# Moving one product and three preparation steps at the hand-over from the written order to the visits

## The chip, the cores and the metric

The kernel runs on one core of one Trainium2 chip. The metric is the device time of one execution in microseconds (us); lower is better. Several runs of the same kernel are taken, and their median is compared. A profile of one further execution shows what each engine did and when.

## The reference

The program chains a recurrent attention block (RetNet) and a feed-forward block with SiLU. All tensors are float32, apart from the weights, which the host hands over as 64-bit floats and the kernel reads as pairs of 32-bit words.

```python
# q, k, v: (B, H, S, D) = (4, 8, 768, 64); w_in: (512, 2048); w_out: (2048, 512)
gamma = 1.0 - 2.0 ** (-5.0 - np.arange(H))
for t in range(S):
    state = gamma[None, :, None, None] * state + einsum('bhd,bhe->bhde', k[:, :, t], v[:, :, t])
    y[:, :, t] = einsum('bhd,bhde->bhe', q[:, :, t], state) / sqrt(D)
x = y.transpose(0, 2, 1, 3).reshape(B * S, H * D)     # 3072 tokens x 512
h = x @ w_in
out = (h * sigmoid(h)) @ w_out
```

## The kernel before

**Tiling.** The sequence is cut into 6 chunks of 128 positions. A *unit* is one chunk of one of the 4 batches: units 0 to 3 are chunk 0, units 4 to 7 are chunk 1, and so on to unit 23. The four units of a chunk make a *group* of 512 tokens, whose x is one tile `xt[c]`. w_in is cut into 16 *slices* of 128 columns. A *product* (c, f) multiplies group c's x by slice f; (1, 0) is group 1 and slice 0.

**Precision.** Each float32 operand is split into three parts, so a product is three groups of four matmuls of 128x512: four for the high part, four for the low part (both add up in the bank `ha`), four for the third part (bank `hb`), all at L645. The x of a unit is split by `split_x`: high part on ScalarE (ACT, L552), low part on VectorE (DVE, L555), third part on DVE (L558). A slice of w_in is first turned from 64-bit to 32-bit floats (`convert_steps`: L196 on ACT, then L199 to L217 on DVE) and then split (`split_steps`: L120 on ACT, L123 on DVE, L126 on ACT, L128 on DVE).

**What a unit goes through.** Its k and q are turned on TensorE (PE) by `stage_t`, called T (L436: `kp` and `qp`), and copied out by ACT (L438). SC makes the scores and the sums (L462, L452), A masks them (L470), adds the state (L478, L482), and Q scales q (L403). `stage_y`, called YA and YB, makes the output y (L501) in two halves. X takes y out (L539, tile `ys`) and splits it into x. K (L398 on DVE) or KA (eight small multiplications on ACT) scales k. A *visit* m in `halves(m)` does T of unit m and the first half of y of unit m-2; after a `yield` it does SC and A of unit m-1, the second half of y and X of unit m-2, issues loads, and handles slices of w_in.

**A product's close.** `close_steps` takes `ha` out on ACT (L655), subtracts `hb` on DVE (L660) and applies SiLU on ACT (L665). The result is a tile `g`; `put_g` writes it to DRAM (L671), from where a second phase reads it back for the multiplication by w_out.

**Shared buffers.** Three PSUM banks, taken in turn by `turn`, hold every `kp`, `ha` and `hb`, so each tile waits until the one three places before it has been read. `qp` has one bank of its own. Three SBUF buffers (`hpool`) hold every `g` and every `ys` in turn, so each waits for the store, or the reader, of the one three places before it. Two landing buffers hold raw slices of w_in; the conversion works in one buffer of each kind.

**What sets the order.** PE runs in the order in which the source calls it. For the other engines the order is the source's as well up to `early_order.close()`; after that a scheduler at build time orders them, with `queue(...)` as hints. The written part ends with T(9), KA(9), the steps of unit 8, X(7), and `begin_w()` for slice 3. From there the list `pairs` names six products with a half visit behind each: `next(half_visits)` runs the first half of visit 10 ahead of the list, and then each product of `pairs` is followed by the next half; the last is followed by the whole of visit 13. The list `three` goes on from there.

**Slices 3 to 6.** `begin_w()` issues a slice's load ahead (two slices on) and its conversion; `end_w()`, called in the next visit, issues its split. Slice 3 is begun in the written part.

```python
        if EARLY + 2 <= m < 3 * B + 2:      # visits 10 to 13
            with queue(masked[0]):
                end_w()
                if EARLY + 2 < m:           # from visit 11
                    begin_w()
```

So visit 10 ends slice 3; visits 11, 12 and 13 begin slices 4, 5 and 6, and visit 12 ends slice 4, visit 13 slice 5. The product (0, 4) stands behind visit 12.

Of the kernel before, what the change touches and what calls it, by code (L numbers as in the profile page):

```python
# [33 lines left out]
def kernel(  # L34
# [29 lines left out]
    B, H, S, D = q.shape  # L64
# [5 lines left out]
    NF = DF // 128  # L70
# [60 lines left out]
    def split_w(*of):  # L131
        steps = split_steps(*of)
        next(steps)
        yield
        list(steps)
# [4 lines left out]
    EARLY = 2 * B  # L140
# [4 lines left out]
    def load(name, n):  # L145
        if n >= len(units):
            return
        c, b = units[n]
        src = {"k": k, "q": q, "v": v}[name]
        if n < EARLY:  # L150

            if n not in early:
                early[n] = wpool.tile([128, 3, H, D], FP32, tag=f"w{4 + n}", name=f"kqv_{n}")
            t = early[n][:, "kqv".index(name)]
        else:
            t = ld.tile([128, H, D], FP32, tag=f"{name}f", name=f"{name}f_{n}",
                        bufs=2 if name == "q" else 3)
        nc.sync.dma_start(out=t, in_=src[b, :, ds(c * C, C)].rearrange("h t d -> t h d"))
        kqv[name][n] = t
# [60 lines left out]
    def convert_w(i):  # L220

        if i + W_AHEAD not in staged:
            load_w(i + W_AHEAD)
        out = []
        steps = convert_steps(i, out)
        for _ in range(6):
            next(steps, None)

        def rounded():
            list(steps)  # L230
            return out[0]

        return rounded
# [53 lines left out]
    def begin_w():  # L287

        i = taken[0]
        taken[0] += 1  # L290
        split = split_w(i, convert_w(i)(), "wi", scale, w_sb, True)
        next(split)
        half_split.append(split)
# [135 lines left out]
    def stage_t(n):  # L429

        for name, to, bufs, src, tp in (
                ("kt", kt, 2, kqv["k"][n], turn(f"kp_{n}")),
                ("qt", qt, 3, kqv["q"].pop(n), banks("q", f"qp_{n}", 1)[:, 0])):
            tp = tp.rearrange("p (a t) -> p a t", a=HP)
            for a in range(HP):
                nc.tensor.transpose(tp[:, a, :], src[:, 2 * a : 2 * a + 2, :], ident)  # L436
            to[n] = one.tile([128, HP, C], FP32, tag=name, name=f"{name}_{n}", bufs=bufs)
            evac[:] = [nc.scalar.copy(out=to[n], in_=tp).ins]  # L438

    def score_tile(n):  # L440
        u = banks("s", f"sc_{n}")
        sc, sums = (u[:, :, ts(i, 4 * D)].rearrange("p o (a t) -> p o a t", a=HP)
                    for i in range(2))
        return sc, sums

    def stage_s(n, sums):

        kf, vs = kqv["k"].pop(n), kqv["v"][n]
        for a in range(HP):
            for o in range(2 if units[n][0] < NC - 1 else 1):  # L450
                for j in range(2):
                    nc.tensor.matmul(sums[ts(j, D), o, a, :], lhsT=kf[ts(o, D), 2 * a + j, :],  # L452
                                     rhs=vs[ts(o, D), 2 * a + j, :], start=True, stop=True,
                                     skip_group_check=True)
# [36 lines left out]
    def stage_y(n):  # L491

        vs, amn, qtn = kqv["v"].pop(n), am.pop(n), qt.pop(n)
        states = steps_of.pop(n)
        yp = banks("y", f"y_{n}")[:, :, : 4 * D].rearrange("p o (a t) -> p o a t", a=HP)

        started, done, new = set(), [], []

        def product(a, o, j, lhsT, rhs):
            e = j ^ (a % 2)  # L500
            i = nc.tensor.matmul(yp[ts(e, D), o, a, :], lhsT=lhsT, rhs=rhs,  # L501
                                 start=(e, o) not in started, stop=True,
                                 skip_group_check=True).ins
            started.add((e, o))
            if new:
                fence(done[-1], i)
                new.clear()
            done.append(i)

        def scores():  # L510
            for a in range(HP):
                for o in range(2):
                    for j in range(2):
                        product(a, o, j, vs[ts(o, D), 2 * a + j, :], amn[ts(o, D), j, a, :])

        def states_with(part):

            new.extend([part] * part)
            for a in range(HP):
                for o in range(2):  # L520
                    j = o ^ part
                    if states[o] is not None:
                        product(a, o, j, states[o][ts(j, D), a, :], qtn[ts(j, D), a, ts(o, D)])

        return scores, states_with, yp
# [67 lines left out]
    def halves(m):  # L593

        first, mid, last = (0 <= m - i < len(units) for i in range(3))
        if first and m < FAR:
            stage_t(m)
        if last:
            scores, states_with, yp = stage_y(m - 2)
            scores()  # L600
            states_with(0)
        yield
        if mid:
            sc, sums = score_tile(m - 1)
            stage_s(m - 1, sums)
            stage_a(m - 1, sc)
            if 1 < m <= 3 * B + 1 and units[m - 1][1] == 0:
                next_chunk()

            with queue(taken_out[0]) if m > 3 * B + 1 else ExitStack():  # L610
                finish_a(m - 1, sc, sums)
            scale_q(m - 1)
            if m > 3 * B + 1 and units[m - 1][1] == B - 1:

                behind_copy.append(next_chunk)
        if first and m < FAR:
            scale_k(m)
        if last:
            states_with(1)
            finish_y(m - 2, yp)  # L620

        if FAR <= m < len(units):
            with queue(fenced[0]):
                part_t(m)
        for name in "kqv":
            for n in (m + 1, m + 2):
                if n >= EARLY and n == (m + 1 if name == "v" or n > FAR else m + 2):
                    load(name, n)
        if EARLY + 2 <= m < 3 * B + 2:
            with queue(masked[0]):  # L630
                end_w()
                if EARLY + 2 < m:
                    begin_w()


# [5 lines left out]
    def multiply(c, f):  # L641
        ha, hb = turn(f"ha_{c}_{f}"), turn(f"hb_{c}_{f}")
        for i in range(3):
            for kk in range(KIN):
                nc.tensor.matmul(hb if i == 2 else ha, lhsT=w_sb[f][:, i, ts(kk, 128)],  # L645
                                 rhs=xt[c][:, i, kk, :], start=kk == 0 and i != 1,
                                 stop=kk == KIN - 1 and i != 0)
        return ha, hb
# [4 lines left out]
    def close_steps(c, f, ha, hb):  # L653
        hs = hpool.tile([128, NT], FP32, tag="hs", name=f"g_{c}_{f}")
        copied[:] = [nc.scalar.activation(out=hs, in_=ha, func=AF.Copy, scale=ONE_E).ins]  # L655
        with queue(copied[0]):
            while behind_copy:
                behind_copy.pop(0)()
        yield
        taken_out[:] = [nc.vector.tensor_tensor(out=hs, in0=hs, in1=hb, op=ALU.subtract).ins]  # L660
        with queue(taken_out[0]):
            while behind_next:
                behind_next.pop(0)()
        yield
        nc.scalar.activation(out=hs, in_=hs, func=AF.Silu)  # L665
        pending.append((c, f, hs))
# [58 lines left out]
    def T(n):  # L725
        stage_t(n)
# [7 lines left out]
    def A(n):  # L734
        next(asteps[n], None)
# [10 lines left out]
    def X(n):  # L746
        next(ysteps[n], None)
# [13 lines left out]
    K, Q = scale_k, scale_q  # L761
# [32 lines left out]
    loads(EARLY - 2), loads(EARLY - 1)  # L794
    closing = {}

    def P(f):
        closing[f] = close_steps(0, f, *multiply(0, f))

    def CL(f):  # L800
        next(closing[f], None)

    def KA(n):
        t = kqv["k"][n]
        for h in range(H):
            nc.scalar.activation(out=t[:, h, :], in_=t[:, h, :], func=AF.Copy,
                                 scale=gk[:, units[n][0], h : h + 1])
# [54 lines left out]
    X(6), X(6)  # L862
    T(9)
    load("v", EARLY + 2), load("k", EARLY + 3), load("q", EARLY + 3)
    KA(9)
    A(8), Q(8), X(7), X(7), A(8)
    taken[0] = 3
    begin_w()
    early_order.close()
    written[0] = False  # L870

# [1 line left out]
    next(half_visits)  # L873

    half = NF // 2
    pairs = [(1, 0), (1, 1), (1, 2), (0, 3), (1, 3), (0, 4)]
    three = [(1, 4)] + [x for f in range(5, half) for x in ((0, f), (1, f), (2, f - 5))]
    rest = ([(2, f) for f in range(half - 5, half)] +
            [(c, f) for c in range(2) for f in range(half, NF - 4)])
    last = ([(c, f) for c in range(2) for f in range(NF - 4, NF)] +  # L880
# [51 lines left out]
    for c in range(NC):  # L932
# [9 lines left out]
        for f in range(NF):  # L942
            n = c * NF + f
# [21 lines left out]
        for b in range(B):  # L965
# [11 lines left out]
            n = 2 if b == B - 1 else 1  # L977
# [36 lines left out]
```

## Time and profile before

| | us |
|---|---|
| median of 5 runs | 627.55 |
| lowest and highest of them | 624.81, 628.99 |
| the profiled execution's own time | 628.35 |
| its span, first to last instruction | 626.4 |
| PE matmuls busy | 605.7 (97% of the span) |
| DVE busy | 424.0 (68%) |
| ACT busy | 312.5 (50%) |
| mean granted PE clock | 0.993 of full |

All views of the profile are of that one execution. Times in them count from its first instruction. In a timeline a row is a run of equal instructions: start, length, engine, source line, operation, output and inputs, and in brackets how long the engine sat idle before it and whose end released it. Matmul ends are modelled, so that rows of PE overlap slightly; starts are the safer numbers.

### The profile page before, as it was taken

What the parts mean: (1) busy time and instruction counts of PE and PEld (TensorE: products, weight loads), DVE (VectorE), ACT (ScalarE), POOL (GpSimd) and SP (SyncE); (2) the same over time, 40 slices, a digit from 0 to 9 for tenths busy, and PEclk for the clock granted to TensorE, in tenths of its full rate; (3) what the DMA queues carried; (4) which work ended last, traced back from release to release, by engine and by line L of the source; (5) the groups of instructions that cost most, each with busy time, mean ns of one, the idle gap of its engine ahead of it and who ended that gap; (6) DMA issues with size and microseconds to landing.
All of it is one profiled execution on the core that took longest, in us unless ns stands there. A gap on an engine that the chain in (4) does not pass through costs nothing.

```text
span 626.4 us, 13491 instructions
## 1 busy us (share of the span) xinstructions
PE 605.7 (97%) x5384; PEld 500.6 (80%) x5384; DVE 424.0 (68%) x731; ACT 312.5 (50%) x595; POOL 22.0 (4%) x79
## 2 busy tenths in 40 slices
PE   6897989999999999999999999999999999999997
PEld 5776867888888888888888888888888888888886
DVE  4897789888979887777599783553635544554631
ACT  6666886666656566566588661322312221312311
POOL 3000000000000221111000000000000000000000
PEclk9898999999999999999999999999999999999999
DMA  9997867645578799999867643342533523342301
GB/s 189 217 224 175 221 180 223 189 158 170 171 218 231 205 259 246 233 261 253 297 225 239 216 134 102 118 151 68 167 102 103 167 81 121 135 129 77 130 1 67
DMA packets 137998, 107.31 MB, mean 171 GB/s; under 512 B 94800, under 2 KB 103248, under 8 KB 137936
## 3 DMA queue, kind: packets, MB, share of 16 engines
q1 hardware_dynamic: 135056, 101.21, 57.3%
q10 hardware_dynamic: 2880, 5.24, 2.3%
q8 instruction: 42, 0.69, 0.5%
q14 instruction: 20, 0.16, 0.1%
HBM read 66.06 MB, written 36.70 MB: 164 GB/s over the span
## 4 chain that ended last, share of the span: by engine, by line
PE 91%; DVE 3%; ACT 2%; DMA 1%; issue 1%; SPq 0%; POOL 0%; DVEq 0%; POOLq 0%; ACTq 0%
PE ha L645 27%; PE o L954 20%; PE oa L954 14%; PE hb L645 13%; PE ob L954 7%; PE y L501 4%; PE sc L452 2%; PE sc L462 2%; DMA gd<-g 1%; PE qp L436 1%; PE kp L436 1%; DVE am L470 1%; PE o L962 0%; ACT ys L539 0%; SPq L180 0%
## 5 line engine op out<-in xcount | busy, mean ns | idle before, releaser
L645 PE MATMUL ha<-xt,wi 128*128 128x512 f32 x768 | 194.5, 395 | 2.4 <-ACT wi L120 2.0
L645 PEld LDWEIGHTS ha<-xt,wi 128*128 128x128 f32 x768 | 142.8, 189 | 34.1 <-ACT wi L120 2.1
L954 PE MATMUL o<-wo,gs 128*128 128x512 f32 x564 | 143.3, 390 | 0.0
L954 PEld LDWEIGHTS o<-wo,gs 128*128 128x128 f32 x564 | 105.9, 188 | 21.8
L712 DVE TENSOR_TENSOR gs<-gr,gs 128x512 fp32r<-128x512 f32 x96 | 62.2, 686 | 90.3 <-ACT gs L710 90.3
L710 ACT ACTIVATE gs<-gr 128x512 fp32r<-128x512 f32 x96 | 53.6, 621 | 134.2 <-issue 131.8
L954 PE MATMUL oa<-wo,gs 128*128 128x512 f32 x376 | 115.8, 390 | 0.0
L645 PE MATMUL hb<-xt,wi 128*128 128x512 f32 x384 | 103.0, 390 | 0.5 <-ACT g L655 0.5
L660 DVE TENSOR_TENSOR g<-g,hb 128x512 f32<-128x512 f32 x96 | 65.7, 685 | 47.0 <-ACT g L655 30.2
L665 ACT ACTIVATE g<-g 128x512 f32<-128x512 f32 x96 | 60.4, 629 | 49.5 <-DVE g L660 49.5
L645 PEld LDWEIGHTS hb<-xt,wi 128*128 128x128 f32 x384 | 72.0, 188 | 16.1 <-ACT g L655 1.2
L954 PEld LDWEIGHTS oa<-wo,gs 128*128 128x128 f32 x376 | 70.6, 188 | 14.7
L954 PE MATMUL ob<-wo,gs 128*128 128x512 f32 x188 | 73.7, 392 | 0.0
L655 ACT ACTIVATE g<-ha 128x512 f32<-128x512 f32 x96 | 56.8, 592 | 32.7 <-PE ha L645 14.4
L713 DVE SCALAR_TENSOR_TENSOR gs<-gs 128x512 fp32r<-128x512 f32 x96 | 62.1, 685 | 0.0
L954 PEld LDWEIGHTS ob<-wo,gs 128*128 128x128 f32 x188 | 35.3, 188 | 8.6 <-DVE o L972 1.6
L196 ACT ACTIVATE ca<-wf 128x512 f32<-128x512 f32 x32 | 21.3, 667 | 6.9 <-DVE cw L217 6.3
L470 DVE TENSOR_TENSOR am<-sc,decay 128x512 f32<-128x512 f32 x24 | 16.5, 687 | 9.8 <-PE sc L462 9.5
L212 DVE SCALAR_TENSOR_TENSOR ca<-wf,ca 128x512 f32<-128x512 uint32 x32 | 22.7, 710 | 0.5
L206 DVE SCALAR_TENSOR_TENSOR cs<-ca,cs 128x512 uint32<-128x512 uint32 x32 | 22.1, 692 | 0.9
L971 ACT ACTIVATE o<-o 128x512 f32<-128x512 f32 x10 | 6.0, 598 | 33.4 <-PE o L954 33.0
L501 PE MATMUL y<-qt,mid 64*64 64x64 f32 x384 | 20.8, 227 | 1.5 <-POOL token L377 0.8
(92 smaller groups left out, 566.6 us busy)
## 6 DMA issues: line engine op xcount, KB each, us to landing
gd<-g SPq DMA_DIRECT2D x96, 256.0 KB, 3.1
gr<-gd SPq DMA_DIRECT2D x96, 256.0 KB, 2.7
wf<-in_moe_w_out_dram SPq DMA_DIRECT2D x16, 512.0 KB, 4.8
out_dram<-o ACTq DMA_DIRECT2D x20, 256.0 KB, 2.1
wf<-in_moe_w_in_dram SPq DMA_DIRECT2D x16, 256.0 KB, 4.1
wf<-in_moe_w_in_dram SPq DMA_DIRECT2D x32, 128.0 KB, 3.8
kf<-in_k_dram SPq DMA_DIRECT2D x16, 256.0 KB, 5.3
qf<-in_q_dram SPq DMA_DIRECT2D x16, 256.0 KB, 4.1
```

The costliest lines, as they stand in the source:

```text
L206: nc.vector.scalar_tensor_tensor(out=s, in0=a, scalar=3, in1=s, op0=ALU.logical_shift_left, op1=ALU.bitwise_or)
L212: nc.vector.scalar_tensor_tensor(out=p.bitcast(FP32), in0=lo, scalar=2.0 ** -52, in1=p.bitcast(FP32), op0=ALU.mult, op1=ALU.mult)
L470: mask = nc.vector.tensor_tensor(out=am[n], in0=sc, in1=decay, op=ALU.mult).ins
L501: i = nc.tensor.matmul(yp[ts(e, D), o, a, :], lhsT=lhsT, rhs=rhs, start=(e, o) not in started, stop=True, skip_group_check=True).ins
L645: nc.tensor.matmul(hb if i == 2 else ha, lhsT=w_sb[f][:, i, ts(kk, 128)], rhs=xt[c][:, i, kk, :], start=kk == 0 and i != 1, stop=kk == KIN ...
L655: copied[:] = [nc.scalar.activation(out=hs, in_=ha, func=AF.Copy, scale=ONE_E).ins]
L660: taken_out[:] = [nc.vector.tensor_tensor(out=hs, in0=hs, in1=hb, op=ALU.subtract).ins]
L665: nc.scalar.activation(out=hs, in_=hs, func=AF.Silu)
L710: nc.scalar.activation(out=t[:, 0, :], in_=g, func=AF.Copy, scale=HALF)
L712: nc.vector.tensor_tensor(out=t[:, 1, :], in0=g, in1=high, op=ALU.subtract)
L713: nc.vector.scalar_tensor_tensor(out=t[:, 2, :], in0=t[:, 1, :].bitcast(FP32), scalar=-1.0 / EPS, in1=high, op0=ALU.mult, op1=ALU.add)
L954: nc.tensor.matmul(o, lhsT=g, rhs=wo[f][:, i, :], start=f == 0 and i != 1, stop=f == NF - 1 and i != 0)
```

## The change

Three edits, all around the hand-over.

1. The first product of group 1, (1, 0), is taken out of `pairs` and written out behind T(9), ahead of visit 10. Its three closing steps (`CL(NF)`, with NF = 16) stand around KA(9) and `begin_w()`. Every later product of `pairs` moves up by one half visit, and (1, 4) comes from `three` into `pairs`.
2. The two last steps of x of unit 7 (`X(7), X(7)`: L555 and L558) stand ahead of A(8), Q(8), A(8).
3. Visits 10, 11 and 13 begin a slice, in place of 11, 12 and 13. So slices 4 and 5 begin (and are split) one visit sooner; slice 6 stays with visit 13.

```diff
         if EARLY + 2 <= m < 3 * B + 2:
             with queue(masked[0]):
                 end_w()
-                if EARLY + 2 < m:
+                if m != 3 * B:
                     begin_w()
...
-    def P(f):
-        closing[f] = close_steps(0, f, *multiply(0, f))
+    def P(n):
+        c, f = divmod(n, NF)
+        closing[n] = close_steps(c, f, *multiply(c, f))
...
     load("v", EARLY + 2), load("k", EARLY + 3), load("q", EARLY + 3)
+    X(7), X(7)
+    A(8), Q(8), A(8)
+    P(NF)
     KA(9)
-    A(8), Q(8), X(7), X(7), A(8)
+    CL(NF)
     taken[0] = 3
     begin_w()
+    CL(NF), CL(NF)
     early_order.close()
...
-    pairs = [(1, 0), (1, 1), (1, 2), (0, 3), (1, 3), (0, 4)]
-    three = [(1, 4)] + [x for f in range(5, half) for x in ((0, f), (1, f), (2, f - 5))]
+    pairs = [(1, 1), (1, 2), (0, 3), (1, 3), (0, 4), (1, 4)]
+    three = [x for f in range(5, half) for x in ((0, f), (1, f), (2, f - 5))]
```

No instruction is added or removed: the counts of matmuls, of ACT and DVE operations and of DMAs are the same.

## The prediction

> **What bounds the kernel now.** The page comes first, its busy row.
>
> ```profile
> PE 605.7 (97%) x5384; PEld 500.6 (80%) x5384; DVE 424.0 (68%) x731; ACT 312.5 (50%) x595; POOL 22.0 (4%) x79
> ```
>
> PE is busy for 605.7 of 626.4 us, so it can gain at most the 20.7 us in which it stands still, and a change of order can gain only what stands still near it. The second view is the waits of PE: engine and line, what it waited for, us in total, times, the longest.
>
> ```profile
> PE y L501 <- ACT ys L539: 4.4, 2, 3.6
> PE kp L436 <- POOL step L342: 4.2, 1, 4.2
> PE ha L645 <- ACT wi L120: 2.0, 1, 2.0
> ...
> PE qp L436 <- ACT qt L438: 0.9, 1, 0.9
> ...
> PE hb L645 <- ACT g L655: 0.5, 1, 0.5
> PE ha L645 <- ACT wi L126: 0.5, 1, 0.5
> ```
>
> The third view, the timeline of PE, says where these lie.
>
> ```profile
> 54.74 1.13 PE L501 MATMUL y<-am,kqv 64*64 64x64 f32 x32 [3.62 <-ACT ys L539]
> ...
> 60.72 0.66 PE L436 MATMUL qp<-ident,qf 128*128 128x128 f32 x4 [0.89 <-ACT qt L438]
> ...
> 86.37 1.21 PE L645 MATMUL ha<-xt,wi 128*128 128x512 f32 x4 [1.95 <-ACT wi L120]
> 88.06 1.20 PE L645 MATMUL ha<-xt,wi 128*128 128x512 f32 x4 [0.48 <-ACT wi L126]
> ...
> 101.40 1.21 PE L645 MATMUL hb<-xt,wi 128*128 128x512 f32 x4 [0.54 <-ACT g L655]
> ```
>
> The largest, 3.62 at 54.74, lies before the first moved instruction (T(9) starts at 58.31) and stays. From T(9) on only four are left: 0.89 (T(10) wants the one `qp` bank while unit 9's q is still being copied), 1.95 and 0.48 (product (0, 4) waits for slice 4), 0.54 (product (1, 5) waits for a bank whose reader waits for a store). After 101.4 the chain that ended last is PE alone for hundreds of us. So the change can gain at most 0.89 + 1.95 + 0.48 + 0.54 = 3.86 us, 0.6%.
>
> **The parts: what is removed.** *The wait of 0.89.* (1, 0) now runs between T(9) and T(10), 2.7 us long (four matmuls take 0.91, as the `hb` rows show), while the copy of q ends at 60.08 + 0.59 = 60.7. Gone.
>
> *The waits of 1.95 and 0.48.* Slice 3 shows the time from a split to its end: visit 10's second half leaves PE at 66.4, and its L126 ends at 70.6, 4.2 us on. Slice 4's split now goes behind visit 11, whose second half leaves PE at about 78.5 (new times), so it ends near 82.7. (0, 4) stands behind the first half of visit 12: 78.5 + 2.95 for (1, 3) + 1.8 = 83.2, and wants the low part at 84.2. Cover 1.5 us: gone, with (1, 3) as what hides it.
>
> *The wait of 0.54.* (0, 5)'s tile now follows unit 10's `ys` three places on, whose store goes out a visit sooner, where it followed (0, 4)'s. Gone; it may come back at (2, 0), whose bank is read after (1, 5)'s tile, which follows (1, 4)'s store: 0 to 0.5. I take 0, because in the built order that store stands before unit 11's `ys` in SP's queue, where the late one (97.45, landed 100.7) stood behind it.
>
> **What is added.** *(1, 0) waits for its own x.* ACT and DVE near T(9):
>
> ```profile
> 59.08 0.63 ACT L552 ACTIVATE xt<-ys 128x512 fp32r<-128x512 f32 x1
> ...
> 60.56 2.03 ACT L806 ACTIVATE kf<-kf,gk 128x64 f32<-128x64 f32 x8
> 62.48 0.68 ACT L196 ACTIVATE ca<-wf 128x512 f32<-128x512 f32 x1
> ```
>
> ```profile
> 60.93 0.69 DVE L555 TENSOR_TENSOR xt<-ys,xt 128x512 fp32r<-128x512 f32 x1
> 61.65 0.69 DVE L558 SCALAR_TENSOR_TENSOR xt<-xt 128x512 fp32r<-128x512 f32 x1
> ...
> 65.57 0.69 DVE L217 TENSOR_TENSOR cs<-cs,ca 128x512 f32<-128x512 f32 x1
> 66.18 0.68 DVE L660 TENSOR_TENSOR g<-g,hb 128x512 f32<-128x512 f32 x1
> ```
>
> T(9) leaves PE at 59.24. The high part of unit 7 is there at 59.7: 0.46 idle. X(7) moves past mid (0.33) and Q (0.60), so L555 runs 60.0 to 60.7 and L558 ends at 61.4. The second four start at 60.7 rather than 60.6 (0.1), the last four at 61.6 wait for nothing. Together 0.57. The mask, state and Q(8) end 1.3 us later, by 62.4 for Q; YA(8) wants them at 63.9, so that costs nothing.
>
> *A bank is free later.* Three banks turn, and the tiles now come as `ha`, `hb` of (1, 0), `kp` of unit 10, `ha`, `hb` of (1, 1): the last takes the bank of `hb` of (1, 0). (1, 0) ends at 62.5, T(10) and YA(8) take 1.84 (69.30 to 71.13 in visit 11), `ha` of (1, 1) starts at 64.4 and `hb`, 1.95 on, at 66.3. The bank is free when L660 of (1, 0) ends. In the built program DVE has the whole conversion of slice 3 (L199 to L217) ahead of that L660; and ACT has L655 of (1, 0) ahead of L196, on which the conversion waits: 62.48 + 0.53 = 63.0. So the DVE rows shift by 0.53: L660 runs 66.7 to 67.4. New wait: 67.4 - 66.3 = 1.1. Bounds: 0.6 if L196 kept its old start, 1.6 if one more step of 0.53 came ahead; I take 1.1, the rows as they are.
>
> The Trainium skill (Perfetto Trace Analysis, Matmuls) says that independent groups should rotate through different PSUM banks, so that the taking-out of one overlaps the matmuls of the next. Read as a promise for these turning banks it would put this term at 0 and the sum at 2.8; the rows of DVE above put work ahead of the taking-out, and I go by them.
>
> *Slice 6 has one product less in front of it.* It is begun in visit 13 as before, but (1, 4) has moved ahead of that visit. Before, visit 13 left PE at 93.0 and L126 of slice 6 ended at 104.32 + 0.63 = 104.95, 11.95 on. Now (0, 6) wants it after three products, 8.3, and 0.9 into its own: 9.2 on. With nothing else changed that is 2.7 of wait. But before, slice 5's split (L123, L128, 1.4 on DVE) and the tile wait at 100.75 (2.2 on ACT) lay in that stretch, and both are gone: 11.95 - 2.2 = 9.75 leaves 0.5, and taking the 1.4 too leaves nothing. Bounds 0 and 2.7; I take 0.5.
>
> *Queues.* SP: the three loads of slice 6 now stand before k of unit 13, waiting for L212 of slice 4 (near 76.8) and holding up k of 13, `ys` of unit 9 and (0, 3)'s store; T(13) wants that k at 90: 0, with 9 us of cover. POOL has 0.09 us fences there, in the same order. ACT: L196 of slice 4 now waits for slice 3's conversion ahead of L655 of (1, 1), L665 of (1, 0) and thus its store; see the last rival.
>
> **Sum.** 3.86 - 0.57 - 1.1 - 0.5 = 1.7 us less. The profiled execution, 628.35, would give 626.65. It lies 0.8 above the median, so the median goes from 627.55 to 625.85. About 0.5% (3.1 us) is what a measurement of this kernel can tell from no change, so the likeliest answer is "the same".
>
> **Rival: the new waits don't form.** If L660 of (1, 0) is early enough and slice 6 too, the sum is 3.86 - 0.57 = 3.3: 624.25, just past 0.5%. For it: 32% of DVE's time is free, and the replaced product pattern, `hb` of (1, 2) on the bank of (1, 1) across half a visit, ran without wait (L660 at 70.55, `hb` at 73.07). Against it: no conversion stood ahead of that L660.
>
> **Rival: it is given back at slice 6.** The full 2.7 there in place of 0.5: 1.7 - 2.2 = 0.5 slower, 628.05. For it: `wi` L120 already set the pace once, with the same chain. Against it: the tile wait of 2.2 that stretched it has lost its cause.
>
> **Rival: slower, by a store that lands late.** The tile of (1, 2) follows that of (1, 0). L665 of (1, 0) moves behind L196 of slice 4 and L655 of (1, 1), to 67.8, its store to 68.5, behind slice 5's loads; before, the store went at 68.98 and L655 of (1, 2) at 74.17. Now L655 wants it at 71.9, 3.4 later. Landing took 2.2 to 5.1 us in this stretch, median 3.2. ACT can wait until 73.6 before `ha` of (0, 3) lacks its bank, so it decides from a landing of 5.1 us. From there each us is a us of PE: beyond 6.8 the kernel is slower than before. A wait as long as the one at 54.74 also halved the clock (x32 took 1.13; the same row at 61.31 takes 0.70) for about 3.4 us, 1.7 us more: 3.6 + 1.7 - 1.7 = 3.6 slower, 631.15. For it: the same mechanism, a store under a tile, made that 3.62. Against it: it needs a landing of 8.7, beyond any seen here.
>
> **How the numbers follow.** Forecast 0.42; no new waits 0.31, as my three added terms rest on modelled PE ends and DVE rows that may move; given back at slice 6 0.15; late store 0.12. The forecast's own range is that of its unknown terms: 0.5 (bank) and 0.5 (slice 6) better, 624.85; 0.5 (bank) and 0.5 (the wait at (2, 0)) worse, 626.85; a slice 6 beyond that is the third case. To leave out 2 in 10 at most, the range goes below the second case by the 1.0 that a median of runs from 624.81 to 628.99 moves, 623.2, and above the third by about as much, 629.0. Faster by over 0.5%: the second case and the forecast's edge, 0.33. Slower by over 0.5%: 0.11. The same: 0.56.
>
> **What would show it.** Right: PE idle at `ha` of (1, 0) with DVE L555 as releaser, about 0.6 in all; at `hb` of (1, 1) <- DVE L660, about 1.1; no wait at T(10) or (0, 4); about 0.5 at (0, 6) <- ACT L126; every PE row after 110 is 1.7 to 2 earlier. Wrong: no wait at `hb` of (1, 1) (second case), a wait over 1 at (0, 6) (third), or a gap at (0, 3) with a `gd` store as its origin and half the clock behind it (fourth).

## The result, and the profile after

The changed kernel takes 624.94 us (median of 28 runs, 622.78 to 628.3), against 627.48 for the kernel before in the same comparison. The ratio is 0.9961, with a 95% interval of 0.9951 to 0.9970: 1.9 to 3.1 us less. The forecast was 1.7 less, 625.85, and "the same" by its mark of 0.5%. The sign is right, the gain of 0.4% lies under that mark, and it passes the forecast by 0.8. With 28 and 52 runs it is clear of no change, since the interval leaves out 1.

The page of the changed kernel, its busy row:

```profile
PE 601.8 (97%) x5384; PEld 496.8 (80%) x5384; DVE 423.3 (68%) x731; ACT 312.9 (50%) x595; POOL 22.5 (4%) x79
```

Its waits of PE (line, what it waited for, us in total, times, the longest):

```profile
PE y L501 <- ACT ys L539: 5.1, 2, 4.8
...
PE hb L645 <- DVE g L660: 0.8, 1, 0.8
...
PE ha L645 <- ACT xt L552: 0.3, 1, 0.3
PE ha L645 <- ACT wi L126: 0.3, 1, 0.3
```

The four waits that the prediction counted are off the list. Two of its three new ones stand on it with the releaser that was named: `hb` for DVE L660 and `ha` for ACT L126. The 0.3 for ACT L552 is not the third: it lies at 27.52, at the first product (0, 0), ahead of every edit. The timeline of PE shows the places near the change:

```profile
53.59 1.13 PE L501 MATMUL y<-am,kqv 64*64 64x64 f32 x32 [4.83 <-ACT ys L539]
58.83 2.14 PE L645 MATMUL ha<-xt,wi 128*128 128x512 f32 x8
...
63.54 2.11 PE L645 MATMUL ha<-xt,wi 128*128 128x512 f32 x8
66.48 1.19 PE L645 MATMUL hb<-xt,wi 128*128 128x512 f32 x4 [0.83 <-DVE g L660]
...
82.60 2.11 PE L645 MATMUL ha<-xt,wi 128*128 128x512 f32 x8
...
98.29 1.98 PE L645 MATMUL ha<-xt,wi 128*128 128x512 f32 x8
...
101.01 1.07 PE L645 MATMUL ha<-xt,wi 128*128 128x512 f32 x4
102.39 1.19 PE L645 MATMUL ha<-xt,wi 128*128 128x512 f32 x4 [0.31 <-ACT wi L126]
...
104.34 1.98 PE L645 MATMUL ha<-xt,wi 128*128 128x512 f32 x8
```

58.83 is (1, 0), without a wait in this profile, 63.54 (1, 1), 82.60 (0, 4) without a wait, 98.29 (2, 0), 101.01 and 102.39 the two halves of `ha` of (0, 6). On ACT and DVE:

```profile
61.59 0.58 ACT L655 ACTIVATE g<-ha 128x512 f32<-128x512 f32 x1
62.06 0.66 ACT L196 ACTIVATE ca<-wf 128x512 f32<-128x512 f32 x1
```

```profile
65.14 0.69 DVE L217 TENSOR_TENSOR cs<-cs,ca 128x512 f32<-128x512 f32 x1
65.75 0.68 DVE L660 TENSOR_TENSOR g<-g,hb 128x512 f32<-128x512 f32 x1
```

This is the new bank wait as it was worked out: L655 of (1, 0), then L196, the conversion, then L660, whose end at 66.43 lets `hb` of (1, 1) start at 66.48.

**Spans of two profiles must not be subtracted here.** 622.7 against 626.4 would be 3.7. But the third product, (0, 2), which lies before every edit, starts at 42.5 in this profile and 44.9 in that of before, and the wait for the store of (0, 1) is 4.83 against 3.62. So a *stretch* is compared below, which holds all the edits and neither of these: from the first transpose of T(9) to the start of the 31st product. It takes 93.13 us before (58.31 to 151.44) and 90.66 after (57.21 to 147.87): 2.5 less, as the medians say. For the same reason the forecast's sign "every PE row after 110 is 1.7 to 2 earlier" can't be read off these two profiles, where the 31st product starts 3.6 earlier.

### The profile page after: what moved, and what is told of

Same layout as the page of the kernel before. It is cut to its first block, busy times and chain, and to the rows that moved or that the text cites. A ratio compares the mean times of both kernels' runs of the same rounds, so it can differ in the third digit from the quotient of the medians.

```text
span 622.7 us, 13496 instructions
## 1 busy us (share of the span) xinstructions
PE 601.8 (97%) x5384; PEld 496.8 (80%) x5384; DVE 423.3 (68%) x731; ACT 312.9 (50%) x595; POOL 22.5 (4%) x79
## 4 chain that ended last, share of the span: by engine, by line
PE 83%; DVE 0%; DVEq 0%; issue 0%; POOLq 0%
PE ha L645 25%; PE o L959 21%; PE oa L959 14%; PE hb L645 12%; PE ob L959 7%; PE y L501 2%; PE sc L462 1%; PE sc L452 1%; PE o L967 0%; PE oa L967 0%; PE qp L436 0%; PE kp L436 0%; PE ob L967 0%; DVE o L985 0%; DVEq L1014 0%
## 5 line engine op out<-in xcount | busy, mean ns | idle before, releaser
L660 DVE TENSOR_TENSOR g<-g,hb 128x512 f32<-128x512 f32 x96 | 65.6, 684 | 39.9 <-ACT g L655 23.1
L645 PEld LDWEIGHTS hb<-xt,wi 128*128 128x128 f32 x384 | 71.9, 188 | 16.5 <-DVE g L660 1.3
L665 ACT ACTIVATE g<-g 128x512 f32<-128x512 f32 x96 | 60.3, 628 | 46.9 <-DVE g L660 46.8
L655 ACT ACTIVATE g<-ha 128x512 f32<-128x512 f32 x96 | 57.0, 593 | 32.0 <-PE ha L645 21.2
L196 ACT ACTIVATE ca<-wf 128x512 f32<-128x512 f32 x32 | 21.4, 669 | 6.8 <-DVE cw L217 5.5
```

The costliest lines, as they stand in the source:

```text
L196: nc.scalar.activation(out=a.bitcast(FP32), in_=hi.bitcast(FP32), func=AF.Abs, scale=65536.0)
```

## The experiments

Each kernel was timed beside the kernel before on its chip. "Stretch" is that of its one profile. Two profiles of one kernel differ in it by 1.1 us (the change and e8) and by 1.7 (e1 and e9), so a smaller difference shows nothing by itself; there the single waits decide.

| kernel | median, before beside it | ratio (95%) | stretch |
|---|---|---|---|
| before | | | 93.13 |
| the change | 624.94, 627.48 | 0.9961 (0.9951 to 0.9970) | 90.66 |
| e1 slices only | 624.58, 627.56 | 0.9947 (0.9930 to 0.9963) | 89.74 |
| e2 x of unit 7 late | 625.76, 627.56 | 0.9973 (0.9957 to 0.9988) | 91.52 |
| e3 close first | 623.37, 627.56 | 0.9937 (0.9914 to 0.9959) | 89.63 |
| e4 slice 5 late | 629.36, 627.56 | 1.0038 (1.0019 to 1.0057) | 95.09 |
| e5 close first, slice 6 early | 625.16, 626.99 | 0.9961 (0.9946 to 0.9976) | 89.99 |
| e6 close first, store first | 622.51, 626.99 | 0.9917 (0.9892 to 0.9942) | 89.58 |
| e7 before, store first | 626.14, 626.99 | 0.9989 (0.9969 to 1.0008) | 93.19 |
| e8 the change again | 625.40, 627.95 | 0.9954 (0.9940 to 0.9968) | 91.80 |
| e9 slices only again | 624.01, 627.95 | 0.9932 (0.9915 to 0.9949) | 91.46 |
| e10 slices only, store first | 621.28, 627.95 | 0.9896 (0.9877 to 0.9914) | 91.03 |

**e1, e9: edit 3 alone.** To the kernel before:

```diff
-                if EARLY + 2 < m:
+                if m != 3 * B:
```

> Before plus edit 3 alone (visits 10, 11 and 13 begin a slice); (1, 0) stays behind visit 10, X(7) stays behind Q(8). Theory (the gain is the sum of PE's waits, and nearly all of it is slice 4's): the 0.89 at T(10) stays, the 1.95 and 0.48 at (0, 4) go, no wait at hb of (1, 1) appears, since (1, 0) still turns the banks the old way; up to 0.7 may come at (2, 0). 2.4 to 3.0 us less than before: 624.5 to 625.1, that is, as fast as the changed kernel or a little faster. Rival (the moved product carries the gain): 1.5 us less at most, 626 or more, with PE waiting elsewhere for slice 4 or 5.

From T(9) on its waits of PE keep the one at T(10) and have none for slice 4, none at `hb`, none at (2, 0) or (0, 6):

```profile
PE qp L436 <- ACT qt L438: 0.5, 1, 0.5
```

The wait at T(10) is printed smaller, but T(9) ran partly at half the clock here: from T(9) to (1, 0) it takes 3.86, as before. The medians differ by 3.0 us (the ratio gives 3.3), at least the gain of the whole change. So the rival that gave the gain to the moved product falls: one line, beginning slices 4 and 5 one visit sooner, is enough for it. No run has edits 1 and 2 without that line. It was run again beside the changed kernel.

> Before plus edit 3 alone, once more beside the changed kernel. Theory (edits 1 and 2 take away 0.89 and bring 1.1 to 1.7, so that edit 3 alone is the better kernel): the same stretch takes 89.5 to 90.1 us, 0.5 to 1 less than the changed kernel's; the median 0.3 to 1 us below it. Rival (edits 1 and 2 are worth something): the stretch is longer than the changed kernel's, and the median is above it.

624.01 against 625.40 on the same chip: 1.4 lower, more than the 0.3 to 1 that was expected, and its stretch is 0.3 shorter (91.46 against 91.80). The direction is that of the theory, but the intervals of the two ratios overlap (0.9915 to 0.9949, 0.9940 to 0.9968), and the stretch itself missed the 89.5 to 90.1 that was expected: in this profile SC(12) in visit 13 waited for the last heads of k on ACT (0.43 shown, `sc` <- `kf` L391), and from (0, 4) to (1, 4) it took 7.50 (83.75 to 91.25) where e1 took 5.85. The scaling of k stands behind L655 of (0, 4) in ACT's order. So edits 1 and 2 together bring no gain that these runs can see; that they cost something is likely and not shown.

**e2: edit 2 undone.**

```diff
-    X(7), X(7)
-    A(8), Q(8), A(8)
+    A(8), Q(8), X(7), X(7), A(8)
     P(NF)
```

> The change without edit 2: X(7) stands behind A(8) and Q(8) again, ahead of the moved product. Theory (the bank wait at hb of (1, 1) swallows what is late ahead of it): (1, 0) waits 0.9 to 1.1 longer for L555 and L558 of unit 7, and the wait at hb of (1, 1) shrinks by the same amount, down to 0 at least; the total moves by 0.5 at most, 625 to 625.5. Rival (edit 2 carries part of the gain by itself): hb of (1, 1) waits as before, 0.8, and the whole 0.9 to 1.1 is lost, 626.

PE's timeline of e2, (1, 0) and `hb` of (1, 1):

```profile
58.53 1.21 PE L645 MATMUL ha<-xt,wi 128*128 128x512 f32 x4 [1.08 <-ACT xt L552]
60.38 1.20 PE L645 MATMUL ha<-xt,wi 128*128 128x512 f32 x4 [0.64 <-DVE xt L555]
...
66.52 1.20 PE L645 MATMUL hb<-xt,wi 128*128 128x512 f32 x4 [0.26 <-DVE g L660]
```

The first row's wait is ACT's, which edit 2 does not touch; the second, 0.64, is the late X(7), and the bank wait behind it is 0.26, where the change has 0.83. So the bank wait gave up 0.57 of the 0.64: what came late ahead of it was waited for there anyway. The median, 625.76, lies between what the theory (625 to 625.5) and the rival (626) gave; 0.8 more than the change is not beyond the two intervals. By these waits, edit 2 is worth what the next wait leaves of it, which here is next to nothing.

**e3: the close of (1, 0) ahead of slice 3's conversion.**

```diff
-    CL(NF)
+    CL(NF), CL(NF)
     taken[0] = 3
     begin_w()
-    CL(NF), CL(NF)
+    CL(NF)
```

> The change, but with the second closing step of (1, 0) (L660 on DVE) ahead of begin_w(), that is ahead of slice 3's conversion on DVE. Theory (the conversion queued ahead of L660 is what makes hb of (1, 1) wait): that wait of 0.8 goes; slice 3 is 0.6 later and has 1.5 us of cover at (0, 3); 0.8 to 1.0 us less than the changed kernel, about 624.0. Rival (the wait is the bank rotation's own, and appears at the next tile, or slice 3 takes its place at (0, 3)): a wait of 0.5 or more at (1, 2) or (0, 3), and the total stays within 0.3 of the changed kernel.

All the waits that PE's timeline of e3 has left after T(9):

```profile
56.90 2.13 PE L645 MATMUL ha<-xt,wi 128*128 128x512 f32 x8 [0.66 <-ACT xt L552]
99.31 1.19 PE L645 MATMUL ha<-xt,wi 128*128 128x512 f32 x4 [0.30 <-ACT wi L126]
```

The wait at `hb` of (1, 1) is gone and nothing came at (1, 2) or (0, 3). From the start of (1, 1) to that of (1, 2) it takes 4.27 in e3, and the same in e5 and e6, which share this order; it takes 5.38 in the change, 5.44 in e8 and 5.26 in e4, which have the conversion first (4.82 in e2, where PE comes later). So the wait's cause is shown: DVE's order, not the rotation of the banks as such. It costs 1.1 us of PE's time, of which 0.83 is printed as idle. The median is 4.2 below before, but its interval overlaps with that of the change, so the total does not show that e3 is the faster one. The Trainium skill's rule (Perfetto Trace Analysis, Matmuls) that groups should rotate through banks was kept in the change too; with the taking-out behind other work of DVE, PE waited 0.83 all the same.

**e4: slice 5 as before.**

```diff
-                if m != 3 * B:
+                if m != 3 * B - 1:
```

> The change with slice 5 begun in visit 12 (so split in visit 13), as before, and slice 4 still in visit 10. Theory (a slice that is split in the visit right ahead of its product makes PE wait): (0, 5), now right behind visit 13, waits 2.4 to 3.4 us for L120 and L126 of slice 5; the wait at (0, 6) goes; 2.3 to 3 us more than the changed kernel, 627.2 to 628, about as slow as before. Rival (what mattered was slice 4 alone; slice 5 has room, because the tile of (0, 5) and its DMA set the time there): within 0.7 us of the changed kernel.

```profile
95.89 3.47 PE L645 MATMUL ha<-xt,wi 128*128 128x512 f32 x8 [3.09 <-ACT wi L120]
99.16 1.61 PE L645 MATMUL hb<-xt,wi 128*128 128x512 f32 x4
```

(0, 5) stands behind visit 13 and waits 3.09 for slice 5, within the 2.4 to 3.4 expected, as (0, 4) behind visit 12 waited for slice 4. The wait at (0, 6) went. The rival (only slice 4 mattered) falls. The total was missed: 4.4 more than the change, where 2.3 to 3 were expected. The rows show the rest: `hb` takes 1.61 and not 1.07, because the granted clock fell to half behind the wait. The windows of e4 (us, PE busy and instructions, granted clock, DMA share, GB/s):

```profile
94.00:96.00 2.00, 0.11 (x1) 1.00 0.49 160
96.00:98.00 2.00, 1.87 (x6) 0.72 0.99 256
98.00:100.00 2.00, 2.00 (x6) 0.50 0.96 275
100.00:102.00 2.00, 2.00 (x10) 0.93 1.04 386
```

**e5: e3 with slice 6 begun one visit sooner.**

```diff
-                if m != 3 * B:
+                if m <= 3 * B:
```

> The kernel with the close first (e3), and slices 4, 5 and 6 begun in visits 10, 11 and 12, none in visit 13. Theory (slice 6 has one product less in front of it, which makes the 0.3 at (0, 6)): that wait goes; but its split then runs on ACT and DVE in visit 13 and behind it, ahead of L655 and L660 of (0, 5) and (1, 5), so that a bank is free later at (1, 5) or (2, 0), 0.2 to 0.8: 0 to 0.5 slower than e3. Rival (slice 6's place is free to choose): the 0.3 goes and nothing comes, 0.3 faster than e3. Either way within 0.5 of it, which the total can't tell: the waits of PE decide.

```profile
99.39 2.11 PE L645 MATMUL ha<-xt,wi 128*128 128x512 f32 x8 [0.38 <-DVE g L660]
```

The wait at (0, 6) went and 0.38 came at (2, 0), for a bank: the theory's trade. Its stretch is 0.4 longer than e3's. Its median is 1.8 below before where e3 had 4.2, far more than the 0 to 0.5 expected. The two intervals overlap, and its profile has a store wait of 5.59 in the first 55 us where e3's has 2.13; whether that is the reason is not shown.

**e8: the changed kernel again.**

> The changed kernel once more, on the same chip as the next two. In its first profile T(9) ran at half the clock, which hid the wait of (1, 0) for its x. Theory (waits of PE alone set the gain, 2.0 to 2.5): in a second profile, from T(9)'s first transpose to the start of the 31st product, 90.1 to 90.9 us against 93.1 before; with T(9) at full clock a wait of 0.4 to 0.7 at ha of (1, 0), and 0.8 to 1.1 at hb of (1, 1). Rival (the first profile was an accident): the stretch differs from 90.7 by over 1 us.

```profile
57.39 2.24 PE L645 MATMUL ha<-xt,wi 128*128 128x512 f32 x8 [0.40 <-ACT xt L552]
65.20 1.20 PE L645 MATMUL hb<-xt,wi 128*128 128x512 f32 x4 [0.88 <-DVE g L660]
102.21 1.19 PE L645 MATMUL ha<-xt,wi 128*128 128x512 f32 x4 [0.40 <-ACT wi L126]
```

Two waits came back in their places, and with T(9) at full clock (1, 0) showed its 0.40. Its releaser is ACT L552. The stretch, 91.80, is 1.1 longer than the first, so it missed the 90.1 to 90.9 and lies just beyond the bound that was set for the rival: 0.5 is in visit 13 and the rest at (2, 0) and (0, 6). So the profile of one run has over 1 us of play in this stretch, and 2.5 for the change is a number of the medians (2.5 in both comparisons), not of one profile.

**e6, e7, e10: the load of slice 4 behind the store of (0, 1).** The largest wait of PE near the change is older than it: y of unit 7 waits for `ys` of unit 6, whose buffer waits for the store of (0, 1). SP's timeline of the kernel before has the load of slice 4 (three DMAs, from 45.44) ahead of that store (48.96), though its tile is written by 46.45 (L665 at 45.83, 0.62 long).

```profile
45.44 1.25 SPq L178 DMA_DIRECT2D wf<-in_moe_w_in_dram  x1
46.73 2.13 SPq L180 DMA_DIRECT2D wf<-in_moe_w_in_dram  x2
48.96 0.55 SPq L671 DMA_DIRECT2D gd<-g  x1
```

```diff
     load("k", EARLY + 1), load("q", EARLY + 1)
-    load_w(4)
...
     CL(1)
     put_g(0)
+    load_w(4)
     T(7)
```

> e3 with one load moved: the load of slice 4 (three DMAs, 3.3 to 4.5 us on SP's queue) is issued behind the store of (0, 1) rather than ahead of it. Theory (the wait of 2.1 to 5.7 us of y of unit 7 for ys of unit 6, which stood before the change and differs from run to run, is that store's: it is issued at 48.4 to 49.8, though its tile is written by 46.5): the store goes out near 46.5 and lands 2 to 3 us sooner; the wait falls to 1 to 2 us, PE's clock is not halved behind it; 2 to 4 us less than e3, 619.5 to 621.5, and a narrower spread. Rival (DMA bandwidth, not the place in the queue, sets when the store lands): the wait stays at 2 to 5 and the total within 1 us of e3.

> Before with the same moved load alone. Theory: the wait of 3.6 at y of unit 7 falls to 1 to 2 us and the half clock behind it goes, 2 to 4 us less than before, 623.5 to 625.5, and the waits of 0.89 at T(10), 1.95 and 0.48 at (0, 4) stay. Rival (what is gained at unit 7 is lost again at T(10) or (0, 4), which wait for ACT and DVE rather than for PE): within 1 us of before, with those waits longer by what was gained.

The wait fell: to 0.43 in e6, to nothing that is printed in e7, and the clock behind it stayed full in both.

```profile
52.84 0.69 PE L501 MATMUL y<-am,kqv 64*64 64x64 f32 x32 [0.43 <-ACT ys L539]
```

The medians moved less than expected, 0.9 in each (e6 against e3 on another chip), and for e7 the interval holds 1. Its waits at T(10) and (0, 4) are 0.45 and 1.95, so they did not grow as its rival said, though the total came out as that rival had it. Nor did the spread narrow: 4.7 us in e6 and 6.0 in e7, where e3 has 4.5. In both profiles (0, 2) started at 46.13, later than in the nine without the edit (42.5 to 45.1). Whether the moved load makes that later was put to e10, which adds the load's move to e1.

> Before plus edit 3, plus the load of slice 4 issued behind the store of (0, 1). What e6 and e7 left open: the wait for that store fell to 0.4 and 0, but the medians fell by 0.9 only. Theory (the store's wait varies from run to run and its gain is real): 1 to 2 us below slices alone, 622.5 to 624, and the third product (0, 2) starts at 42.5 to 45, as in the kernels that issue the load first. Rival (what comes ahead of the store gets later by about as much): (0, 2) starts at about 46 again, as in both kernels with the moved load, and the median is within 0.7 of slices alone.

(0, 2) started at 43.03, so that rival falls. The traces of e6 and e7 say the same: (0, 1) started at 40.3 in both, where the other kernels have 36.7 to 39.3, and that is ahead of anything that the edit moves. The median is 621.28, 2.7 below e9 on the same chip; this is the fastest kernel of the study, 1.0% below before (0.9877 to 0.9914). Its wait at y of unit 7 is 1.92, where e9 has 4.30. Part of the wait has turned into one for k and q of unit 10. The load of that k is issued at 50.68, 0.5 later than in e9, but PE is ready for it at 54.33, where T(10) started at 58.43 in e9:

```profile
55.49 0.63 PE L436 MATMUL kp<-ident,kf 128*128 128x128 f32 x4 [1.16 <-DMA kf<-in_k_dram]
57.35 0.63 PE L436 MATMUL qp<-ident,qf 128*128 128x128 f32 x4 [1.23 <-DMA qf<-in_q_dram]
```

Why e7 gained so little of the same edit (0.9 against 2.7) stays open; its interval reaches to 1.9. In its profile the clock fell to half at (0, 4) (last section), and from there to (1, 4) it took 7.52 where before took 6.63; whether that is so in its other runs is not known.

## Why the prediction was right, and where a size was off

*The sign and the ceiling.* The change could touch only what lies behind T(9), and it did: from the 31st product to the end it is 475.0 us before and 474.9 after. The size of the ceiling, 3.86 us, was too low.

*What was removed.* All four waits went. But 3.86, the sum of their idle times, was too small, because a wait costs PE more than the idle time that is printed. Measured from start to start:

| before | took | the same work without the wait | lost | printed as idle |
|---|---|---|---|---|
| T(9) to (1, 0) | 3.86 (58.31 to 62.17) | 2.76 (0.93, and 1.83 from 69.30 to 71.13) | 1.10 | 0.89 |
| (1, 3) to T(13) behind (0, 4) | 9.93 (80.08 to 90.01) | 7.13 (73.65 to 80.78, after) | 2.80 | 2.43 |
| (1, 5) | 3.57 (98.88 to 102.45) | 2.72 (98.29 to 101.01, after) | 0.85 | 0.54 |

The first row after a wait runs longer (1.19 to 1.21 for four matmuls, where 1.07 is usual), which is part of it. So 4.75 was removed and not 3.86. This is the term that was mis-sized, by 0.9.

*(1, 0) waits for its x: 0.57.* Measured 0.40 in e8 and 0.66 in e3. The releaser there is ACT L552, as the sum had it for 0.46 of the 0.57, and not DVE L555, which was named as the sign. In the first profile after the wait was hidden by an accident: T(9) ran at half the clock (57.21 to 58.83, 1.62, where before it took 0.93), so that 0.69 was lost in its place.

*The bank: 1.1.* 0.83 and 0.88 as idle, and 1.1 from start to start (5.38 for (1, 1), 4.27 in e3); L660 ran from 65.75 to 66.43 in its profile, with the order that was read from the built program. e3 shows the cause.

*Slice 6: 0.5, within 0 and 2.7.* 0.31 and 0.40 as idle; from (0, 6) to the next product 3.33 us (104.34 - 101.01) where 2.72 is usual, so 0.6. (L126 of slice 6 before is 0.61 long and not 0.63, which changes nothing.)

*The sum.* By the profiles 4.75 was removed, and 0.69, 1.11 and 0.61 were added: 2.3 less, of the 2.5 that the stretch and the medians show. The forecast had 3.86 and 2.17. So the mechanism of each term was right, and the gain was larger mainly because idle time was taken for the whole cost of a wait. On the added side 2.41 stands against 2.17, with the half clock of T(9), which was chance, in place of the wait of (1, 0).

*The store that lands late.* It was as near as said, and did not decide: after, L655 of (1, 2) waited 0.99 for a `gd` store and started at 71.9, well ahead of the point at which PE would have noticed. The clock part of that rival was seen in e4. The rival "no new waits" (chance 0.31) falls: the waits at `hb` of (1, 1) and at (0, 6) came in both profiles of the change.

*What the prediction did not see.* Its parts were weighed as one change. By e1 the product's move and X(7) bring nothing on top of edit 3: the 0.89 at T(10) was traded for 0.4 to 0.7 at (1, 0) and 0.8 to 0.9 at (1, 1). The sum had that in it (0.89 against 0.57 and 1.1), but did not draw it out.

## What to carry to other kernels

Issue the work that PE needs early enough: here the split of a slice in the visit right ahead of its product left PE idle for 2.4 us at (0, 4) and for 3.1 at (0, 5), with half the clock behind it, and one line that began it a visit sooner brought as much as the whole change. Price a wait from start to start, not by its idle time. When a product is moved ahead, look at what stands before its closing steps in the orders of DVE and ACT, since the next product waits for its bank. A moved part is worth only what the next wait leaves of it, so take a change of several edits apart before keeping all of them.

## What the runs showed of the hardware that was not expected

The granted clock of PE fell to half behind every single wait over 3 us that these profiles hold after its first matmul (3.09 in e4 to 5.69 in e1). Shorter waits did not settle it: 2.73 in e2 and 1.95 at (0, 4) before left it at full, but behind the same 1.95 in e7 it was 0.56 and 0.59 of full (84 to 86 and 86 to 88), and (0, 4) took this long:

```profile
83.99 3.76 PE L645 MATMUL ha<-xt,wi 128*128 128x512 f32 x8 [1.95 <-ACT wi L120]
```

In the kernel before it was at half around the first product too, behind a row of waits none of which reached 1 us (from 20 us on; the last numbers of a row are granted clock, DMA share and GB/s):

```profile
26.00:28.00 2.00, 1.13 (x11) 0.87 0.88 192
28.00:30.00 2.00, 2.00 (x9) 0.50 0.85 213
```

So no bound for one wait comes out of these runs, and a short wait may cost half the clock in one run and not in the next. After the 4.83 of the changed kernel it stayed low for longer, in the windows of its profile:

```profile
52.00:54.00 2.00, 0.41 (x16) 0.54 1.22 261
54.00:56.00 2.00, 2.00 (x86) 0.50 0.66 112
56.00:58.00 2.00, 2.00 (x52) 0.50 0.38 135
58.00:60.00 2.00, 2.00 (x11) 0.76 0.32 75
```

The Trainium skill (TensorE: Matmul & The Clock Gate, Why this matters for your kernels) asks for no idle gaps of TensorE over about 3 us. The waits over 3 us here agree; the 1.95 of e7 shows that to stay below was not enough.

One and the same wait, y of unit 7 for the store of (0, 1), took 1.84 to 5.69 us over the nine profiles that issue the load first. Whether it makes the spread of a few us between runs of one kernel is not shown. The runs of e6 and e7, in whose profiles that wait is nearly gone, still spread by 4.7 and 6.0 us, which speaks against it.
